# Grouped-query attention on one NeuronCore: the remainder tile of P transposed by DMA instead of TensorE in 101 of 128 steps

## The chip, the cores and the metric

The kernel runs on one core of a Trainium2 chip. The metric is device time in microseconds of one execution; for the kernel before, the median of three runs is given. A profile is one more execution with the hardware profiler on; its span runs from the first to the last instruction, and its own time is a little longer than the span. The engines are TensorE (PE in the profile, its weight loads PEld), VectorE (DVE), ScalarE (ACT), GpSimd (POOL) and SyncE (SP), which issues nearly all the DMA transfers. SPq is SyncE's sequencer.

## The reference

Two independent attention problems, A and B, have the same shapes; their outputs are joined along the last axis.

```python
B, Sq, D = 16, 80, 576
Hq, Hkv, Sk, Dh = 32, 16, 512, 128
...
q = (x @ wq).reshape(B, Sq, Hq, Dh).transpose(0, 2, 1, 3)
k = jnp.repeat(k_cache, 2, axis=1)
v = jnp.repeat(v_cache, 2, axis=1)
scores = jnp.einsum("bhqd,bhkd->bhqk", q, k) * (Dh ** -0.5)
p = softmax(scores, axis=-1)
o = jnp.einsum("bhqk,bhkd->bhqd", p, v)
return o.transpose(0, 2, 1, 3).reshape(B, Sq, Hq * Dh) @ wo
```

All tensors are bf16. Two query heads share one K/V head. Their 2 x 80 queries make 160 rows of scores by 512 keys for each of 16 batch entries, 16 K/V heads and 2 problems.

## The kernel before

**Units.** A unit U is one batch entry and four K/V heads of it; there are 64 units in each problem, 128 in all (`for U in range(NSU)`, line 573). A unit has four groups of 160 query rows. Since a tile has 128 partitions, each group gives one tile of its first 128 rows, and the last 32 rows of all four groups together make a fifth, the remainder tile. So a unit has five tiles k = 0 to 4: k = 0 is the remainder tile R, k = 1 to 4 are the A tiles. A step T = 5U + k is one tile.

**Loads.** SyncE loads K for a unit with a transposing DMA from HBM (`em_ldk`, line 582: 512 KB into one of NK buffers of `kT`) and V with a plain one (`em_ldv`, line 586: 512 KB into one of NV buffers of `v_sb`). It also loads pieces of wq (lines 487 and 490), wo (552) and x (422; 454 and 458 transposing, for problem B) and stores the output (775). SyncE's instructions run in order; each waits for the semaphores that it needs.

**A tile's way.** TensorE computes scores into PSUM (`em_qkr`, line 613, for the remainder tiles of a pair of units, four matmuls side by side; `em_qk`, line 627, for an A tile). VectorE takes the negated maximum (636), ScalarE the exponential with the row sum (640) into a slot of `p_sb`. When all five tiles of a unit have their sums, VectorE takes one reciprocal of the five columns (646; the groups are given by `RG`), and GpSimd scales each tile by it (649). TensorE transposes the tile with four matmuls against an identity (`em_tr`, 655), VectorE copies it from PSUM into `pT` (661 for the remainder tile, 663 for an A tile). Then TensorE multiplies with V (`em_pv`, 693: for each group four matmuls of 160 columns, 128 from its A tile and 32 from the remainder tile), and ScalarE copies the result to `oT` (708). Around this run the projection of Q (513, copied by 524 or 525) for the units to come, and the output projection (741, added up by 753, 764 or 769).

**Buffers.** `p_sb` has NPA = 9 slots for A tiles and NPR = 4 for remainder tiles, `pT` has NPT = 2 buffers of a unit each, `kT` NK = 6, `v_sb` NV = 4. PSUM has eight banks, given out by class (`BANKS`).

**Order.** The order of every engine's instructions is fixed when the program is built. Each operation has a due time (key) in steps, a duration, a list of what it reads and writes, and a stream; `_Sched.arrange` (line 115) is a list scheduler that walks through time, takes for each engine the ready operation with the lowest key among the heads of its streams, and gives out PSUM banks. For DMA it keeps one server, whose costs are constants (KC for a K load, VC for a V load, WQC for wq). `finalize` (229) turns the order into semaphore waits. LA is the number of steps by which the scores of a tile are due ahead of its transposition. Units are taken in pairs (GR = 2): the scores of both remainder tiles first, then the eight A tiles.

The layout of `pT` before is [128, buffer, group, j, 160], where j counts the four blocks of 128 keys:

```python
def em_ptev(e, k=k, gl=gl, vt=vt, pts=pts):
    if k == 0:
        return e.tensor_copy(pT[:, pts, :, :, 128:160],
                             psb[:, vt.phys, 0:512].rearrange("p (j g c) -> p g j c", j=4, g=4))
    return e.tensor_copy(pT[:, pts, gl, :, 0:128],
                         psb[:, vt.phys, 0:512].rearrange("p (j n) -> p j n", j=4))
```

Of the kernel before, what the change touches and what calls it, by code (L numbers as in the profile page):

```python
# [13 lines left out]
LA = 9  # L14
NK = 6
NV = 4
NPA = 9
NPR = 4
NPT = 2
# [3 lines left out]
KC = 3.1  # L23
# [5 lines left out]
VC = 1.75  # L29
# [11 lines left out]
RG = ((0, 1, 2, 3, 4),)  # L41
# [29 lines left out]
class _Op:  # L71
    __slots__ = ("engs", "eng", "key", "seq", "emit", "reads", "writes", "dsem", "stream", "dur", "lat", "cost",
                 "alloc", "pre", "start", "done", "mode",
# [3 lines left out]
class _Sched:  # L77
# [9 lines left out]
    def add(self, eng, key, emit, reads=(), writes=(), dsem=None, name="", stream=None, dur=0.1, lat=0.15,  # L87
            cost=0.0, alloc=(), mode=0):
        op = _Op()
        op.engs = (eng,) if isinstance(eng, str) else tuple(eng)  # L90
        op.eng = op.engs[0]
        op.key = float(key)
        op.seq = len(self.ops)
# [12 lines left out]
        op.pre = []  # L106
        op.start = op.done = None
        op.signals = False
        op.sidx = None
        op.waits = []  # L110
        op.clock = None
        self.ops.append(op)
        return op

    def arrange(self):
# [33 lines left out]
        mode = 0  # L149
# [5 lines left out]
        def ready(o):  # L155
            t = 0.0
            for d in o.pre:
                if d.done is None:
                    return None
                if not (d.eng == "pe" and o.engs[0] == "pe"):  # L160
                    t = max(t, d.done)
            if o.alloc:
                used = []
                for vb in o.alloc:
                    c = [(bank_free[b], n_, b) for n_, b in enumerate(BANKS[vb.cls])
                         if bank_free[b] is not None and b not in used]
                    if not c:
                        return None
                    b = min(c)
                    used.append(b[2])  # L170
                    t = max(t, b[0])
            return t

        while left:
            best = None
            for e in free:
                cand = []
                for n in by_eng[e]:
                    if at[n] < len(streams[n]):
                        o = streams[n][at[n]]  # L180
                        r = ready(o)
# [12 lines left out]
            dur = o.dur[e] if isinstance(o.dur, dict) else o.dur  # L194
            if e == "pe":
                if o.mode != mode:
                    st = max(st, now + 0.1)
                    mode = o.mode
            if o.alloc:
                used = []  # L200
                for vb in o.alloc:
                    b = min((bank_free[b], n_, b) for n_, b in enumerate(BANKS[vb.cls])
                            if bank_free[b] is not None and b not in used)[2]
                    used.append(b)
                    vb.phys = b
                for b in used:
# [91 lines left out]
def bass_concat_heads__gqa_block_cached__gqa_block_cached__near_ridge_kernel(  # L298
# [27 lines left out]
    with ExitStack() as es:  # L326
# [9 lines left out]
        pT = sb("pT", [128, NPT, 4, 4, 160], BF16)  # L336
# [14 lines left out]
                     + ["d_out%d" % i for i in range(NOSB)]  # L351
                     + ["d_k%d" % i for i in range(NK)] + ["d_v%d" % i for i in range(NV)])
# [115 lines left out]
        for goct in range(NG):  # L468
# [30 lines left out]
            for i in range(8):  # L499
                for c in range(2):  # L500
# [27 lines left out]
                    if prob:  # L528
# [3 lines left out]
                          writes=[R(vb, 0)], name="qp%d.%d.%d" % (goct, i, c), stream="Q",  # L532
# [40 lines left out]
        for U in range(NSU):  # L573
# [19 lines left out]
            vo = None  # L593
            for k in range(5):
# [47 lines left out]

                rg = [g_ for g_ in RG if k in g_][0]

# [28 lines left out]
                if k == rg[-1]:  # L673
                    S.add("dve", tg + 1.85, em_rcp, reads=[R(("rs", ss, k_), U) for k_ in rg],
                          writes=[R(("ri", ss, rg), U)], name="rcp%d" % T, stream="rcp", dur=0.10, lat=0.13)
# [3 lines left out]
                S.add("pe", t0, em_tr, reads=[R(("P", psl), ("n", T)), IDENT], writes=[R(vt, 0)],  # L679
                      name="tr%d" % T, stream="T", dur=_mm(4, 128), lat=0.2, alloc=[vt])  # L680
                S.add("dve", t0 + 0.44, em_ptev, reads=[R(vt, 0)], writes=pt_writes,
                      name="ptev%d" % T, stream="ptev", dur=0.33, lat=0.13)

                if k >= 1:
# [17 lines left out]
                    if gl % 2 == 1:  # L702
                        hb = 8 * (q % 2) + 4 * pr

                        def em_oev(e, vo=vo, hb=hb, row=half * NROW + bl * SQ):
# [6 lines left out]
                              stream="oev", dur=0.33)  # L712
# [4 lines left out]
        for prob in range(2):  # L717
            for hh in range(NPAIR):
                for half in range(NPP):
                    for n in range(NB_):  # L720
# [30 lines left out]
                        if hh == 0:  # L751
                            def em_ea(e, rb=rb, c3=c3, vb=vb):
# [5 lines left out]
                                  stream="oea", dur=0.30)  # L758
                        elif not last:
                            def em_em(e, rb=rb, c3=c3, vb=vb):  # L760
# [5 lines left out]
                                  stream="oeb", dur=0.38)  # L766
                        else:
# [4 lines left out]
                            def em_st(e, rb=rb, c3=c3, prob=prob, slot=slot):  # L772
# [6 lines left out]
                                  stream="oeb", dur=0.38)  # L779
# [75 lines left out]
```

## Time and profile before

| | |
|---|---|
| median of three runs | 790.78 us (790.53 to 791.19) |
| the profiled execution | 791.1 us |
| its span | 789.1 us, 21625 instructions |
| granted TensorE clock | 1.000 |
| share of the span on the chain that ended last | PE 87%; DVE 9% |
| line 655 in that chain | 16% |
| GpSimd scaling (649) | 640 of 692 ns |
| ScalarE exponentials (640) | 640 of 693 ns, 640 sum reads of 203 ns |
| VectorE maxima (636) | 640 of 677 ns |
| copies to pT (663 / 661) | 512 of 411 ns / 128 of 414 ns |
| reciprocals (646) | 128 of 179 ns |
| transposing matmuls (655), matmuls with V (693) | 2560, 2048 |
| K load, issue to landing | median 5.9 us (4.2 to 10.2) |
| V load, issue to landing | median 4.7 us (3.8 to 7.8) |
| DMA in all | 160.56 MB, mean 203 GB/s; q1 busy for 88.8% of 16 engines' span |

How to read it: a row of a group names the source line, engine, operation, output and inputs with shapes and count, then busy time and the mean length of one in ns, then the idle time of the engine before them and what ended it. Matmuls overlap, so the mean length of one is more than what it takes of the engine; the distance from one start to the next tells that. DMA shares are the time that packets took over 16 engines' time. A row of a timeline has the start, the length and the work, merged where the same work follows itself. For SyncE the length is that of issuing, with what holds it back.

### The profile page before, as it was taken

What the parts mean: (1) busy time and instruction counts of PE and PEld (TensorE: products, weight loads), DVE (VectorE), ACT (ScalarE), POOL (GpSimd) and SP (SyncE); (2) the same over time, 40 slices, a digit from 0 to 9 for tenths busy, and PEclk for the clock granted to TensorE, in tenths of its full rate; (3) what the DMA queues carried; (4) which work ended last, traced back from release to release, by engine and by line L of the source; (5) the groups of instructions that cost most, each with busy time, mean ns of one, the idle gap of its engine ahead of it and who ended that gap; (6) DMA issues with size and microseconds to landing.
All of it is one profiled execution on the core that took longest, in us unless ns stands there. A gap on an engine that the chain in (4) does not pass through costs nothing.

```text
span 789.1 us, 21625 instructions
## 1 busy us (share of the span) xinstructions
PE 782.3 (99%) x8258; PEld 577.7 (73%) x8258; DVE 687.8 (87%) x1553; ACT 613.9 (78%) x1741; POOL 432.1 (55%) x647
## 2 busy tenths in 40 slices
PE   9999999999999999999999999999999999999998
PEld 5677767777777777777777777777777777777776
DVE  4999999988888889889989999998888898989974
ACT  1779989888778889777787778888788877877852
POOL 1456666565564565565555555655555655654633
DMA  9999999999797899999988779998778876999620
GB/s 244 230 244 220 243 215 251 239 228 201 174 209 177 191 227 269 248 207 228 198 194 177 187 181 253 250 243 227 174 169 173 190 167 161 263 246 181 158 77 24
DMA packets 362085, 160.56 MB, mean 203 GB/s; under 512 B 276096, under 2 KB 358528, under 8 KB 361984
## 3 DMA queue, kind: packets, MB, share of 16 engines
q1 hardware_dynamic: 360768, 158.00, 88.8%
q8 instruction: 67, 1.10, 0.6%
q10 hardware_dynamic: 1216, 1.18, 0.4%
q14 instruction: 34, 0.28, 0.1%
HBM read 87.46 MB, written 2.95 MB: 115 GB/s over the span
## 4 chain that ended last, share of the span: by engine, by line
PE 87%; DVE 9%; SPq 1%; DMA 1%; ACT 1%; POOL 1%; issue 0%
PE ps L741 20%; PE ps L513 18%; PE ps L655 16%; PE ps L693 16%; PE ps L627 12%; DVE negmax L636 5%; PE ps L613 4%; DVE pT L663 2%; SPq L582 1%; DVE qT L525 1%; DMA wq_sb<-in_A_wq_dram 1%; POOL p_sb L649 1%; DVE pT L661 0%; ACT p_sb L640 0%; SPq L422 0%
## 5 line engine op out<-in xcount | busy, mean ns | idle before, releaser
L649 POOL TENSOR_SCALAR p_sb<-p_sb,rinv 128x512 bf16<-128x512 bf16 x640 | 429.7, 692 | 342.6 <-DVE rinv L646 342.3
L640 ACT ACTIVATE p_sb<-ps,negmax 128x512 bf16<-128x512 f32 x640 | 441.1, 693 | 84.0 <-DVE negmax L636 75.3
L636 DVE TENSOR_REDUCE negmax<-ps 128x1 f32<-128x512 f32 x640 | 428.4, 677 | 6.1 <-PE ps L627 2.0
L655 PE MATMUL ps<-ident,p_sb 128*128 128x128 bf16 x2560 | 240.7, 219 | 0.9 <-POOL p_sb L649 0.2
L663 DVE COPY pT<-ps 128x512 bf16<-128x512 bf16 x512 | 207.8, 411 | 19.9 <-PE ps L655 18.3
L693 PE MATMUL ps<-pT,v_sb 128*128 128x160 bf16 x2048 | 216.2, 233 | 0.5 <-ACT oT L708 0.3
L513 PE MATMUL ps<-xT,wq_sb 128*128 128x480 bf16 (+1 forms) x1280 | 211.7, 299 | 1.0 <-DVE xT L441 0.6
L655 PEld LDWEIGHTS ps<-ident,p_sb 128*128 128x128 bf16 x2560 | 177.2, 98 | 42.4 <-DVE pT L663 5.9
L693 PEld LDWEIGHTS ps<-pT,v_sb 128*128 128x128 bf16 x2048 | 158.5, 98 | 53.8 <-issue 11.9
L627 PE MATMUL ps<-kT,qT 128*128 128x512 bf16 x512 | 186.5, 379 | 0.0
L741 PE MATMUL ps<-wo_sb,oT 128*128 128x288 bf16 x1280 | 171.6, 286 | 0.5 <-ACT oT L708 0.5
L708 ACT CAST oT<-ps 128x320 bf16<-128x320 f32 x256 | 108.5, 425 | 55.0 <-PE ps L693 54.4
L513 PEld LDWEIGHTS ps<-xT,wq_sb 128*128 128x128 bf16 x1280 | 106.6, 98 | 59.2 <-issue 1.5
L741 PEld LDWEIGHTS ps<-wo_sb,oT 128*128 128x128 bf16 x1280 | 122.4, 98 | 35.0 <-ACT oT L708 1.4
L640 ACT ACTIVATION_READ_ACCUMULATOR p_sb<-ps,negmax 128x1 f32 x640 | 130.0, 203 | 0.0
L524 ACT ACTIVATE qT<-ps 128x160 bf16<-128x160 f32 (+1 forms) x164 | 65.9, 402 | 23.9 <-PE ps L513 23.1
L525 DVE TENSOR_SCALAR qT<-ps 128x480 bf16<-128x480 f32 (+1 forms) x92 | 51.7, 563 | 22.2 <-PE ps L513 21.3
L661 DVE COPY pT<-ps 128x512 bf16<-128x512 bf16 x128 | 53.0, 414 | 8.9 <-PE ps L655 7.4
L627 PEld LDWEIGHTS ps<-kT,qT 128*128 128x128 bf16 x512 | 48.6, 98 | 4.3 <-ACT p_sb L640 1.4
L769 DVE TENSOR_TENSOR osb<-ps,acc 128x288 bf16<-128x288 f32 x40 | 18.2, 456 | 25.4 <-PE ps L741 25.2
L613 PE MATMUL ps<-kT,qT 128*32 128x512 bf16 x512 | 39.6, 384 | 0.0
L646 DVE RECIPROCAL rinv<-rowsum 128x5 f32<-128x5 f32 x128 | 22.9, 179 | 9.9 <-ACT p_sb L640 9.8
(19 smaller groups left out, 48.2 us busy)
## 6 DMA issues: line engine op xcount, KB each, us to landing
v_sb<-in_A_v_cache_dram SPq DMA_DIRECT2D x64, 512.0 KB, 4.8
v_sb<-in_B_v_cache_dram SPq DMA_DIRECT2D x64, 512.0 KB, 4.7
wo_sb<-in_A_wo_dram SPq DMA_DIRECT2D x8, 576.0 KB, 6.7
wo_sb<-in_B_wo_dram SPq DMA_DIRECT2D x8, 576.0 KB, 7.1
wq_sb<-in_B_wq_dram SPq DMA_DIRECT2D x4, 1024.0 KB, 6.6
out_dram<-osb SPq DMA_DIRECT2D x40, 72.0 KB, 2.3
wq_sb<-in_A_wq_dram SPq DMA_DIRECT2D x2, 1024.0 KB, 6.3
wq_sb<-in_A_wq_dram ACTq DMA_DIRECT2D x2, 512.0 KB, 6.8
```

The lines of the kernel that those rows point to most:

```text
L513: last = e.matmul(ps[:, vb.phys, 0:n1 - n0], lhsT=wq_sb[:, wsl, ck, i * 128:(i + 1) * 128], rhs=xT[:, half, ck, n0:n1], start=(ck == 0), s ...
L524: return e.activation(dst, src, AF.Identity, scale=SCALE)
L613: last = e.matmul(ps[32 * g4:32 * g4 + 32, vb_.phys, :], lhsT=qT[:, qsl_, bl_, g4 * 160 + 128:g4 * 160 + 160], rhs=kT[:, ks_, :, g4 * 128: ...
L627: return e.matmul(ps[:, vb.phys, :], lhsT=qT[:, qsl, bl, gl * 160:gl * 160 + 128], rhs=kT[:, ks, :, gl * 128:(gl + 1) * 128], start=True, ...
L636: return e.tensor_reduce(negmax[:, si:si + 1], ps[:, vb.phys, :], axis=AX.X, op=AluOpType.max, negate=True)
L640: return e.activation(p_sb[:, psl, :], ps[:, vb.phys, :], AF.Exp, bias=negmax[:, si:si + 1], scale=1.0, accum_out=rowsum[:, ss, k:k + 1])
L649: return e.tensor_scalar(p_sb[:, psl, :], p_sb[:, psl, :], rinv[:, ss, k:k + 1], 1.0, op0=AluOpType.mult, op1=AluOpType.mult)
L655: last = e.transpose(psb[:, vt.phys, j * 128:(j + 1) * 128], p_sb[:, psl, j * 128:(j + 1) * 128], ident[:])
L663: return e.tensor_copy(pT[:, pts, gl, :, 0:128], psb[:, vt.phys, 0:512].rearrange("p (j n) -> p j n", j=4))
L693: last = e.matmul(ps[:, vo.phys, off:off + 160], lhsT=v_sb[:, vs, gl, j * 128:(j + 1) * 128], rhs=pT[:, pts, gl, j, :], start=(j == 0), st ...
L708: return e.copy(dst, src)
L741: last = e.matmul(ps[:, vb.phys, 0:DC], lhsT=oT[:, hi, rb * 128:(rb + 1) * 128], rhs=wo_sb[:, wi, c3 * DC:(c3 + 1) * DC], start=(hi == 0), ...
```

## The change

For units 24 to 124 (the condition takes U from 24 on and below 125, U % 2 being 0 or 1), the remainder tile is no longer transposed by TensorE and copied by VectorE. SyncE issues a transposing DMA from the tile's slot of `p_sb` in SBUF to its place in `pT`, also in SBUF. In these units the remainder tile has a reciprocal of its own, and the four A tiles share another. The layout of `pT` becomes [128, buffer, j, 5, 128]: for each block of keys four runs of 128 for the A tiles, cut as 32 rows of each of the four groups, and a fifth for the remainder tile. So a copy of an A tile writes runs of 32, and a matmul with V reads its 160 columns as five runs of 32. `pT` gets three buffers, K five instead of six, the A tiles of `p_sb` eight instead of nine, LA is 10 instead of 9, and two of the scheduler's DMA costs are lower.

The scheduler also changes how it gives out PSUM banks (the first bank of the class that is free at the time, tried for all banks that an operation needs, instead of the one that came free first), an operation may be put ahead of its key by `ahead` (used, with 6.0, for the new DMA alone: the others are 0.0), and the Q projection's matmuls also count as writers of `qT`.

```diff
-LA = 9
-NK = 6
+LA = 10
+NK = 5
 NV = 4
-NPA = 9
+NPA = 8
 NPR = 4
-NPT = 2
+NPT = 3
...
-KC = 3.1
+KC = 2.95
...
-VC = 1.75
+VC = 1.65
...
-RG = ((0, 1, 2, 3, 4),)
+RG = (((0, 1, 2, 3, 4),), ((0,), (1, 2, 3, 4)))
+RDMA = (24, 125)
+RPER = (0, 1)
+RSKIP = ()
+RDC = 0.75
+RDK = 3.0
+RDO = 6.0
+RDD = 0.8
...
+        def pick(vbs, now, used=()):
+            if not vbs:
+                return []
+            c = sorted((max(bank_free[b], now), n_, b) for n_, b in enumerate(BANKS[vbs[0].cls])
+                       if bank_free[b] is not None and b not in used)
+            for t, n_, b in c:
+                r = pick(vbs[1:], now, used + (b,))
+                if r is not None:
+                    return [(t, b)] + r
+            return None
...
-            k_, s_, r, o = min(((o.key, o.seq, r, o) for r, o in cand if r <= now + hold[e]), key=lambda x: x[:2])
+            k_, s_, r, o = min(((o.pri, o.seq, r, o) for r, o in cand if r <= now + hold[e]), key=lambda x: x[:2])
...
-        pT = sb("pT", [128, NPT, 4, 4, 160], BF16)
+        pT = sb("pT", [128, NPT, 4, 5, 128], BF16)
...
-                          writes=[R(vb, 0)], name="qp%d.%d.%d" % (goct, i, c), stream="Q",
+                          writes=[R(vb, 0)] + [R(("qT", qsl, bl, i), goct) for bl in range(b0, b0 + nb)],
+                          name="qp%d.%d.%d" % (goct, i, c), stream="Q",
...
+            rdma = RDMA[0] <= U < RDMA[1] and U % 2 in RPER and not any(a_ <= U < b_ for a_, b_ in RSKIP)
...
-                rg = [g_ for g_ in RG if k in g_][0]
+                rg = [g_ for g_ in RG[rdma] if k in g_][0]
...
                     if k == 0:
-                        return e.tensor_copy(pT[:, pts, :, :, 128:160],
-                                             psb[:, vt.phys, 0:512].rearrange("p (j g c) -> p g j c", j=4, g=4))
-                    return e.tensor_copy(pT[:, pts, gl, :, 0:128],
-                                         psb[:, vt.phys, 0:512].rearrange("p (j n) -> p j n", j=4))
+                        return e.tensor_copy(pT[:, pts, :, 4, :],
+                                             psb[:, vt.phys, 0:512].rearrange("p (j n) -> p j n", j=4))
+                    return e.tensor_copy(pT[:, pts, :, 0:4, gl * 32:gl * 32 + 32],
+                                         psb[:, vt.phys, 0:512].rearrange("p (j h c) -> p j h c", j=4, h=4))
+
+                def em_rtr(e, psl=psl, pts=pts):
+                    return e.dma_start_transpose(pT[:, pts, :, 4, :], p_sb[:, psl, :])
...
+                if k == 0 and rdma:
+                    S.add("sp", max(tg + RDK, 5.0 * (U - NPT) + 7.0), em_rtr, reads=[R(("P", psl), ("n", T))], writes=pt_writes, dsem="d_r%d" % pts,
+                          name="rtr%d" % T, stream="RT", dur=RDD, cost=RDC, ahead=RDO)
+                else:
+                    S.add("pe", t0, em_tr, reads=[R(("P", psl), ("n", T)), IDENT], writes=[R(vt, 0)],
+                          name="tr%d" % T, stream="T", dur=_mm(4, 128), lat=0.2, alloc=[vt])
+                    S.add("dve", t0 + 0.44, em_ptev, reads=[R(vt, 0)], writes=pt_writes,
+                          name="ptev%d" % T, stream="ptev", dur=0.33, lat=0.13, ahead=PTO)
...
                             lhsT=v_sb[:, vs, gl, j * 128:(j + 1) * 128],
-                                            rhs=pT[:, pts, gl, j, :], start=(j == 0), stop=(j == 3))
+                                            rhs=pT[:, pts, j, :, gl * 32:gl * 32 + 32], start=(j == 0), stop=(j == 3))
```

More of the change, by code (lines that the diff above doesn't have):

```diff
@@ L40 @@
 XDMA = True
-RG = ((0, 1, 2, 3, 4),)
+RG = (((0, 1, 2, 3, 4),), ((0,), (1, 2, 3, 4)))
[6 more added lines that the diff above has]
+RDD = 0.8
+PTO = 0.0
+OEO = 0.0
+OVO = 0.0
+QEO = 0.0
+RCO = 0.0
 NSS = 6
@@ L72 @@
     __slots__ = ("engs", "eng", "key", "seq", "emit", "reads", "writes", "dsem", "stream", "dur", "lat", "cost",
-                 "alloc", "pre", "start", "done", "mode",
+                 "alloc", "pri", "pre", "start", "done", "mode",
                  "deps", "signals", "sidx", "waits", "clock", "name")
@@ L87, in add @@
     def add(self, eng, key, emit, reads=(), writes=(), dsem=None, name="", stream=None, dur=0.1, lat=0.15,
-            cost=0.0, alloc=(), mode=0):
+            cost=0.0, alloc=(), mode=0, ahead=0.0):
         op = _Op()
@@ L92, in add @@
         op.key = float(key)
+        op.pri = op.key - ahead
         op.seq = len(self.ops)
@@ L153, in arrange, with ready @@
         hold = dict(pe=0.05, dve=0.02, act=0.02, pool=0.0, sp=0.0)
-        def ready(o):
+        def pick(vbs, now, used=()):
[8 more added lines that the diff above has]
+            return None
+        def ready(o, now):
             t = 0.0
@@ L162, in ready @@
             if o.alloc:
[L163 to L171, printed above, removed]
+                c = pick(o.alloc, max(t, now))
+                if c is None:
+                    return None
+                t = max([t] + [bank_free[b] for _, b in c])
             return t
@@ L180, in arrange @@
                         o = streams[n][at[n]]
-                        r = ready(o)
+                        r = ready(o, free[e])
                         if r is not None:
@@ L195, in arrange @@
             if e == "pe":
-                if o.mode != mode:
+                if o.mode and mode == 0 or o.mode != mode:
                     st = max(st, now + 0.1)
-                    mode = o.mode
+                mode = o.mode
             if o.alloc:
[L200 to L204, printed above, removed]
+                for vb, (_, b) in zip(o.alloc, pick(o.alloc, max(r, now))):
                     vb.phys = b
-                for b in used:
                     bank_free[b] = None
@@ L351, in bass_concat_heads__gqa_block_cached__gqa_block_cached__near_ridge_kernel @@
                      + ["d_out%d" % i for i in range(NOSB)]
+                     + ["d_r%d" % i for i in range(NPT)]
                      + ["d_k%d" % i for i in range(NK)] + ["d_v%d" % i for i in range(NV)])
@@ L674, in bass_concat_heads__gqa_block_cached__gqa_block_cached__near_ridge_kernel @@
                     S.add("dve", tg + 1.85, em_rcp, reads=[R(("rs", ss, k_), U) for k_ in rg],
-                          writes=[R(("ri", ss, rg), U)], name="rcp%d" % T, stream="rcp", dur=0.10, lat=0.13)
+                          writes=[R(("ri", ss, rg), U)], name="rcp%d" % T, stream="rcp", dur=0.10, lat=0.13, ahead=RCO)
                 S.add("pool", tg + 2.0 + 0.01 * k, em_nrm,
@@ L678, in bass_concat_heads__gqa_block_cached__gqa_block_cached__near_ridge_kernel @@
                       writes=[R(("P", psl), ("n", T))], name="nrm%d" % T, stream="pool", dur=0.674, lat=0.1)
[L679 to L682, printed above, removed]
+                if k == 0 and rdma:
[6 more added lines that the diff above has]
+                          name="ptev%d" % T, stream="ptev", dur=0.33, lat=0.13, ahead=PTO)
                 if k >= 1:
@@ L711, in bass_concat_heads__gqa_block_cached__gqa_block_cached__near_ridge_kernel @@
                               writes=[R(("oT", half, bl, q % 2, pr), (prob, q // 2))], name="oev%d.%d" % (U, pr),
-                              stream="oev", dur=0.33)
+                              stream="oev", dur=0.33, ahead=OEO)
         NB_ = NRT * NOC
@@ L757, in bass_concat_heads__gqa_block_cached__gqa_block_cached__near_ridge_kernel @@
                                   name="oea%d.%d.%d" % (prob, half, n),
-                                  stream="oea", dur=0.30)
+                                  stream="oea", dur=0.30, ahead=OVO)
                         elif not last:
@@ L765, in bass_concat_heads__gqa_block_cached__gqa_block_cached__near_ridge_kernel @@
                                   writes=[R(("acc", rb, c3), ver)], name="oem%d.%d.%d.%d" % (prob, hh, half, n),
-                                  stream="oeb", dur=0.38)
+                                  stream="oeb", dur=0.38, ahead=OVO)
                         else:
@@ L778, in bass_concat_heads__gqa_block_cached__gqa_block_cached__near_ridge_kernel @@
                                   writes=[R(("osb", slot), (prob, half, n))], name="oeb%d.%d.%d" % (prob, half, n),
-                                  stream="oeb", dur=0.38)
+                                  stream="oeb", dur=0.38, ahead=OVO)
                             S.add("sp", xe + 0.3, em_st, reads=[R(("osb", slot), (prob, half, n))],
```

## The prediction

> **What bounds the kernel now.** I read the page's busy times first, then its groups of instructions.
>
> ```profile
> PE 782.3 (99%) x8258; PEld 577.7 (73%) x8258; DVE 687.8 (87%) x1553; ACT 613.9 (78%) x1741; POOL 432.1 (55%) x647
> ...
> L655 PE MATMUL ps<-ident,p_sb 128*128 128x128 bf16 x2560 | 240.7, 219 | 0.9 <-POOL p_sb L649 0.2
> ```
>
> TensorE is busy 782.3 of 789.1 us; the next engine, VectorE, 687.8. A transposing matmul (L655) is given as 219 ns, but they overlap: 2,560 times 219 ns would be 561 us, and their busy time is 240.7. What one costs TensorE shows in TensorE's timeline (start, length, work):
>
> ```profile
> 307.41 0.39 PE L655 MATMUL ps<-ident,p_sb 128*128 128x128 bf16 x4
> 307.63 0.38 PE L627 MATMUL ps<-kT,qT 128*128 128x512 bf16 x1
> ```
>
> The four transposes of one tile start at 307.41, the next matmul at 307.63: one tile costs 0.22 us of TensorE. So TensorE's sequence of matmuls sets the end, and a tile taken from it is worth 0.22 us as long as nothing else makes TensorE wait.
>
> Next I asked how near the second resource is, the DMA engines that bring K and V. The view by stages gives for each stretch the busy times of the engines, then the granted clock, the DMA engines' share and GB/s:
>
> ```profile
> 40.00:183.00 143.00, 142.20 (x1538) 103.40 (x1531) 131.96 (x301) 125.63 (x361) 87.27 (x131) 1.00 1.08 233
> 183.00:736.00 553.00, 552.61 (x5904) 412.02 (x5902) 491.65 (x1108) 443.16 (x1261) 310.68 (x463) 1.00 0.91 206
> ```
>
> TensorE does not idle in the long stage (552.61 of 553), at clock 1.00 in both rows. The DMA engines stand at 1.08 in the early stage (packets overlap, so full load reads a little over 1) and at 0.91 in the later one. SyncE's own timeline says the same:
>
> ```profile
> 139.25 7.05 SPq L582 DMA_TRANSPOSE kT<-in_A_k_cache_dram  x2
> 146.35 0.59 SPq L586 DMA_DIRECT2D v_sb<-in_A_v_cache_dram  x1
> 146.98 4.09 SPq L582 DMA_TRANSPOSE kT<-in_A_k_cache_dram  x1
> 151.12 0.58 SPq L586 DMA_DIRECT2D v_sb<-in_A_v_cache_dram  x1
> 151.75 3.78 SPq L582 DMA_TRANSPOSE kT<-in_A_k_cache_dram  x1
> 155.57 1.13 SPq L586 DMA_DIRECT2D v_sb<-in_A_v_cache_dram  x2
> 156.76 8.21 SPq L582 DMA_TRANSPOSE kT<-in_A_k_cache_dram  x2
> 165.02 1.67 SPq L586 DMA_DIRECT2D v_sb<-in_A_v_cache_dram  x2
> 166.73 4.89 SPq L582 DMA_TRANSPOSE kT<-in_A_k_cache_dram  x1
> 172.04 0.37 SPq L586 DMA_DIRECT2D v_sb<-in_A_v_cache_dram  x1
> 172.47 4.26 SPq L582 DMA_TRANSPOSE kT<-in_A_k_cache_dram  x1
> 176.78 0.58 SPq L586 DMA_DIRECT2D v_sb<-in_A_v_cache_dram  x1
> 177.40 4.66 SPq L582 DMA_TRANSPOSE kT<-in_A_k_cache_dram  x1
> ...
> 202.47 2.32 SPq L582 DMA_TRANSPOSE kT<-in_A_k_cache_dram  x1
> 204.83 0.58 SPq L586 DMA_DIRECT2D v_sb<-in_A_v_cache_dram  x1
> 208.37 2.06 SPq L582 DMA_TRANSPOSE kT<-in_A_k_cache_dram  x1
> ```
>
> From 139.25 to 177.40 SyncE issues without a break and is held back: 8 K loads and 8 V loads in 38.15 us, 4.77 us a pair. That is what the DMA engines supply at full load. Later there are holes: after the V load of 204.83 the next K load starts at 208.37, because it waits for TensorE to free its K buffer. So from 183 us on the loads wait for TensorE. How far ahead they are, by the line of problem B's K loads in the view of line 582 (count, shortest, median and longest issue in ns, first and last start):
>
> ```profile
> L582 SPq DMA_TRANSPOSE kT<-in_B_k_cache_dram x64: 1310/2901/7492, 359.1 to 730.4; - x64
> ```
>
> The last K load starts at 730.4; the same view gives a median of 5.9 us from issue to landing, so it lands at 736.3; TensorE's timeline has its first reader (L613) at 756.50. It could come 20.2 us later for nothing.
>
> **The change, part by part.**
>
> *Removed.* The condition takes every unit from 24 to 124, even and odd: 101 remainder tiles. TensorE loses 101 x 0.22 = 22.2 us. VectorE loses 101 copies of 414 ns (row L661, like L663's 411), 41.8 us.
>
> *Added on VectorE.* 101 further reciprocals, 128x1 where the row L646 has 128x5 at 179 ns: at most 101 x 0.18 = 18 us, at least nothing. I take 18; VectorE ends at 688 - 42 + 18 = 664 us, well under TensorE. At the upper end nothing changes. ScalarE and GpSimd do the same 640 tiles as before; GpSimd's wait for the reciprocal (342 us in all) shows room there.
>
> *Same price, other place.* The pT layout changes: L663's copies now write runs of 32 elements and L693's matmuls read 160 columns in five such runs. For the copy the trace has both forms: runs of 32 in L661, 414 ns, against runs of 128 in L663, 411: nothing. For the matmul the nearest row is L627, whose 512 columns come in four runs of 128: started at 307.63, followed at 307.85, so 0.22 us for 512 columns, no visible loss. Bounds 0 and, at 4 ns for each of 2,048 matmuls, 8 us; I take 0.
>
> *LA 9 to 10, NK 6 to 5, NPA 9 to 8, the bank picker.* These move the order, not the amount of work. The scores run one tile earlier, a K buffer is released about a unit (6 us) later relative to its load. K loads were up to some 25 us early in the quiet stage, so I take 0; it costs up to 6 us where they are late already. Below nothing: the few TensorE gaps left before the last stage could close, at most 782.3 against 789.1 us, of which most is the start; 2 us.
>
> *Added on SyncE and the DMA engines.* 101 transposes of 128 KB each, a quarter of a K load. No row shows a transfer from SBUF to SBUF. Nearest row: K loads issued back to back while held back, 7.05 us for two at 139.25, so about 3.4 us each. Bounds: a quarter of the shortest K issue (1.31 us), 0.33 us, and a whole one, 1.31 us, if most of it does not shrink with the size. I take a little under the quarter of 3.4 us, since the pair of 139.25 queued behind V loads too: 0.78 us, 79 us in all.
>
> One rule speaks against this step. The Trainium skill, "VectorE: DVE Perf Modes", section "The three transpose paths", lists 1309 ns for a 128x128 transpose by DMA and 390 ns on TensorE. This trace differs for both: 0.055 us a block at TensorE's pace (0.22 over four), and 0.21 us a block for a K load (3.4 us over its 16 blocks). By the page's figure a remainder tile would take an estimated 5.2 us of DMA, 529 us in all, and the kernel would run hundreds of us longer. I go by the rows.
>
> *What hides the 79 us.* Only the spare time of the DMA engines from 183 to 736 us. Two readings. By SyncE: 93 K loads follow from 183.41 on, 93 x 4.77 = 444 us; the other transfers, at K's 3.4 or V's 4.77 - 3.4 = 1.4 us per 512 KB, are 12 wo pieces 19, four wq loads 13, two x transposes 11, some 20 stores 4, together 47; 444 + 47 = 491 of 547 us, 56 spare. By the stages: (1 - 0.91/1.08) x 553 = 87 us. The middle is 71.
>
> *Sum.* The last K load lands at 736.3 + 79 - 71 = 744. TensorE wants it at 756.5 - 22.2 = 734. So TensorE waits about 10 us somewhere before, and this wait is the new price. The profiled execution took 791.1 us around its span of 789.1: 791.1 - 22.2 + 10 = 778.9. The median of the runs, 790.78, lies 0.3 lower, so **779 us**.
>
> *The new wait.* On SyncE a transpose waits for GpSimd's normalization, and nearly each also for the PV matmuls (L693) of three units before, which free its pT buffer. In the changed order two units read V, R, K, R, V, K: a K and a V load stand behind each R. Their readers have the leads above as cover. PV itself now waits for the landing. In TensorE's timeline of before, PV of unit 71 ended at 447.50 and PV of unit 74 began at 462.07, 14.6 us later; the transpose needs its place behind one K issue (2 to 5 us) and about 5.9 us to land, 11 at most. When K issues take 7 us, as at some places, little is left.
>
> **The rivals.**
>
> *Hidden entirely.* If an R costs 0.6 us, its share by bytes of a pair (128 KB of 1 MB, 4.77/8), 61 us fit into 71 spare and no wait appears: 791 - 22 = 769; with closed gaps 767. For it: SyncE stood idle in many holes after 183 us. Against it: holes are wanted evenly, and the stages with wo, wq and x loads have none.
>
> *The DMA engines become the bound (slower).* Place: the K loads of the crowded stages, from about unit 50 on. Price: at 0.88 us an R (a quarter of 3.5) and 56 us spare the last K load lands at 736.3 + 89 - 56 = 769, 35 us after it is wanted: 791 - 22 + 35 = 804. It turns slower once transposes minus spare pass 20 us, so at 0.90 us an R with the middle spare, or 0.75 with the lower one. For it: the SyncE reading of 4.77 us a pair, and one buffer of K less. Against it: the stages' reading.
>
> *It does not do what it says.* If the matmuls read runs of 32 more slowly, say 7 ns on each of 2,048, PV takes 14 us back and with the wait of the forecast nothing is left: 779 + 14 = 793. Row L627 speaks against it.
>
> **How the numbers follow.** Forecast, part of the gain given back to DMA waits: 0.46 (its own range 771 to 788). Hidden: 0.25. DMA the bound: 0.23, of which 0.02 ends beside the old time. Reads slower: 0.06. The range runs from 766, just under the hidden case, to 801, inside the slower one, leaving out about 0.05 above and little below; the far ends of an R's price, 0.33 us (33 us in all: hidden) and 1.31 us (132 us: a wait of 63 and 832 us), lie in it and above it. A difference under 0.2% (1.6 us) could not be told from none. Faster: 0.46 + 0.25 with a small loss to "same", 0.70; same 0.04; slower 0.26.
>
> **What would show it.** TensorE's transposes 404 fewer and 22 us less of them on the chain; 101 more issues on SyncE, 128 KB each; DMA share in the long stage near 1.05; the holes on SyncE gone; new waits of L613 or L627 for kT, or of L693 for pT, some 10 us in all. No such waits: the hidden case. Waits above 20 us, named kT: the bound has moved. Waits on pT: the landing is late, which I count small. Wrong altogether if PV's pace leaves 0.28 us a group (307.13 to 307.41), or if VectorE becomes the longest.

## The result, and the profile after

The changed kernel takes 812.41 us (median of four runs, 811.29 to 817.73) against 790.65 for the kernel before beside it (790.42 to 791.19): a ratio of 1.0287, 95% interval 1.0242 to 1.0333. It is slower by 21.8 us where 779 was forecast. The profiled execution took 812.9 us, with a span of 811.2.

The page of the kernel after, its busy times, queue q1, the engines' shares of the chain that ended last, and some groups (busy, mean ns of one, then idle time before them and what ended it):

```profile
PE 775.9 (96%) x7854; PEld 554.5 (68%) x7854; DVE 665.0 (82%) x1554; ACT 613.1 (76%) x1740; POOL 432.8 (53%) x647
...
q1 hardware_dynamic: 415712, 171.26, 97.4%
...
PE 67%; DVE 17%; ACT 7%; DMA 7%; issue 1%; POOL 1%; SPq 1%; ACTq 0%
...
L680 DVE COPY pT<-ps 128x512 bf16<-128x512 bf16 x512 | 207.7, 412 | 36.2 <-PE ps L672 34.1
L717 PE MATMUL ps<-pT,v_sb 128*128 128x160 bf16 x2048 | 202.5, 234 | 16.6 <-DMA pT<-p_sb 4.1
...
L672 PE MATMUL ps<-ident,p_sb 128*128 128x128 bf16 x2156 | 204.2, 220 | 4.8 <-POOL p_sb L666 2.8
...
L663 DVE RECIPROCAL rinv<-rowsum 128x1 f32<-128x1 f32 (+1 forms) x229 | 37.3, 164 | 17.3 <-ACT p_sb L657 17.0
```

TensorE lost its 404 transposing matmuls (2560 to 2156) and is busy 6 us less, but in a longer span: 96% where it was 99%. The matmuls with V (L717, before L693) had 0.5 us of idle time before them and now have 16.6; what ended the largest single part of it, 4.1 us, was the new transfer. The part of TensorE in the chain fell from 87% to 67%.

The view by stages of the kernel after (PE, PEld, DVE, ACT, POOL busy; then granted clock, DMA share, GB/s):

```profile
40.00:183.00 143.00, 141.23 (x1503) 101.69 (x1501) 130.96 (x304) 122.87 (x352) 87.95 (x131) 1.00 1.06 234
183.00:736.00 553.00, 529.03 (x5356) 379.24 (x5355) 455.35 (x1074) 430.68 (x1226) 302.52 (x450) 0.99 1.01 217
```

The early stage is nearly as before: TensorE idles 1.8 us in it where it idled 0.8, and experiment 1 below, without the transfers, has 1.7. In the long one TensorE now idles 24 us where it idled 0.4, and the DMA share went from 0.91 to 1.01.

SyncE's timeline of the kernel after, in a stretch without other transfers:

```profile
542.70 3.25 SPq L598 DMA_TRANSPOSE kT<-in_B_k_cache_dram  x1
545.99 1.27 SPq L684 DMA_TRANSPOSE pT<-p_sb  x1
547.31 0.57 SPq L602 DMA_DIRECT2D v_sb<-in_B_v_cache_dram  x1
547.92 3.45 SPq L598 DMA_TRANSPOSE kT<-in_B_k_cache_dram  x1
551.48 1.21 SPq L684 DMA_TRANSPOSE pT<-p_sb  x1
552.73 1.50 SPq L602 DMA_DIRECT2D v_sb<-in_B_v_cache_dram  x1
554.60 3.49 SPq L598 DMA_TRANSPOSE kT<-in_B_k_cache_dram  x1
```

Two units, K, R and V each, take from 542.70 to 554.60, 5.95 us a unit; ten units from 542.70 (the tenth next K load starts at 600.64) make 5.79. A pair of K and V alone took 4.77 at full load, so an R (the new transfer) costs 1.0 to 1.2 us of the supply. The K load behind an R is still held 3.25 to 3.5 us. From 183 to 736 us SyncE's holes of more than 0.2 us add up to 158 us in the kernel before and to 5 in this one. Its last K load and its R lines, from the views of their source lines (shortest, median, longest issue in ns; first and last start), with who waited for an R (us, times) and the time from issue to landing, read:

```profile
L598 SPq DMA_TRANSPOSE kT<-in_B_k_cache_dram x64: 1387/3410/5917, 374.9 to 763.5; - x64
```

```profile
L684 SPq DMA_TRANSPOSE pT<-p_sb x101: 1189/1212/3190, 154.4 to 772.9; - x101
...
who waited for it (us, times):
  ACT p_sb L657: 9.1, 9
  PE ps L717: 4.1, 4
  PEld ps L717: 3.8, 3
...
DMA to landing us min/median/max: 2.4/3.8/8.9
```

The last K load starts at 763.5 where it was 730.4, 33.1 us later, and lands 0.31 us ahead of its reader where there were 20. An R never takes SyncE less than 1.19 us. Not only the matmuls with V wait for it. An R also reads its tile's slot in `p_sb`, one of four, and the exponential (L657) of the remainder tile four units later may not write there before; ScalarE waited 9.1 us for that, in 9 places.

How this reaches TensorE, at one place. First SyncE, then TensorE (the bracket is idle time and what ended it), both of the kernel after:

```profile
404.58 3.11 SPq L598 DMA_TRANSPOSE kT<-in_B_k_cache_dram  x1
407.79 1.21 SPq L684 DMA_TRANSPOSE pT<-p_sb  x1
```

```profile
410.41 0.38 PE L644 MATMUL ps<-kT,qT 128*128 128x512 bf16 x1
412.52 1.21 PE L717 MATMUL ps<-pT,v_sb 128*128 128x160 bf16 x15 [1.72 <-DMA pT<-p_sb]
```

This R's tile had been scaled by 392.89, and its place in pT was free at 395.61. Behind other loads it was issued at 407.79 only, 12.2 us later, landed at 412.47, and TensorE's next matmul waited 1.72 us for it. Matched to its tile by the program's order, each of the 101 R gives such a time from ready to issued: the median is 9.7 us, the longest 20.2.

**An account of TensorE's time.** For every matmul I took the time from its start to the next start, less the pace of its form (0.22 us for 512 columns); what is left is a stall. Before: 15.4 us in all, 1.3 of it ahead of L693. After: 59.0, of which 23.0 ahead of L717, 9.1 ahead of L672, 14.2 ahead of the scores L630 and L644 (6.2 before), 5.9 ahead of L765. So 791.1 (the profiled execution of before) - 22.2 saved + 43.6 more stalls = 812.5, where 812.9 was measured. The sum has to close nearly by itself, since the time from the first matmul to the last is made of paces and stalls; that it does shows that the matmuls kept their paces. So the saving is there, and the added stalls are twice as large. By the program's order some 16 of the 23.0 us ahead of L717 end with the landing of an R; all the waits that end with the landing of a K load come to some 3 us. About 3.4 us of the stalls come from two stretches at half the granted clock (last section); they aren't the cause, for the run of 811.29 us had a granted clock of 1.000.

### The profile page after: what moved, and what is told of

Read it like the earlier page. It is cut to its first block, busy times and chain, and to the rows that moved or that the text cites. A ratio compares the mean times of both kernels' runs of the same rounds, so it can differ in the third digit from the quotient of the medians.

```text
span 811.2 us, 20842 instructions
## 1 busy us (share of the span) xinstructions
PE 775.9 (96%) x7854; PEld 554.5 (68%) x7854; DVE 665.0 (82%) x1554; ACT 613.1 (76%) x1740; POOL 432.8 (53%) x647
## 3 DMA queue, kind: packets, MB, share of 16 engines
q8 instruction: 64, 1.05, 0.5%
## 4 chain that ended last, share of the span: by engine, by line
PE 67%; DVE 17%; ACT 7%; DMA 7%; issue 1%; POOL 1%; SPq 1%; ACTq 0%
PE ps L765 16%; PE ps L528 14%; PE ps L717 13%; DVE negmax L653 10%; PE ps L672 10%; PE ps L644 8%; ACT p_sb L657 5%; DMA pT<-p_sb 5%; DVE pT L680 4%; PE ps L630 3%; DVE qT L540 1%; DMA wo_sb<-in_B_wo_dram 1%; ACT oT L732 1%; DMA out_dram<-osb 1%; ACT qT L539 1%
## 5 line engine op out<-in xcount | busy, mean ns | idle before, releaser
L657 ACT ACTIVATE p_sb<-ps,negmax 128x512 bf16<-128x512 f32 x640 | 439.8, 696 | 76.2 <-DVE negmax L653 59.8
L653 DVE TENSOR_REDUCE negmax<-ps 128x1 f32<-128x512 f32 x640 | 425.6, 678 | 34.9 <-PE ps L630 18.3
L680 DVE COPY pT<-ps 128x512 bf16<-128x512 bf16 x512 | 207.7, 412 | 36.2 <-PE ps L672 34.1
L717 PE MATMUL ps<-pT,v_sb 128*128 128x160 bf16 x2048 | 202.5, 234 | 16.6 <-DMA pT<-p_sb 4.1
L672 PE MATMUL ps<-ident,p_sb 128*128 128x128 bf16 x2156 | 204.2, 220 | 4.8 <-POOL p_sb L666 2.8
L717 PEld LDWEIGHTS ps<-pT,v_sb 128*128 128x128 bf16 x2048 | 152.3, 98 | 61.4 <-ACT p_sb L657 8.5
L644 PE MATMUL ps<-kT,qT 128*128 128x512 bf16 x512 | 185.2, 380 | 2.1 <-ACT p_sb L657 1.9
L672 PEld LDWEIGHTS ps<-ident,p_sb 128*128 128x128 bf16 x2156 | 151.8, 98 | 51.7 <-DVE pT L680 10.4
L765 PE MATMUL ps<-wo_sb,oT 128*128 128x288 bf16 x1280 | 175.6, 288 | 3.6 <-ACT p_sb L657 2.0
L765 PEld LDWEIGHTS ps<-wo_sb,oT 128*128 128x128 bf16 x1280 | 122.4, 98 | 40.0 <-ACT oT L732 2.2
L657 ACT ACTIVATION_READ_ACCUMULATOR p_sb<-ps,negmax 128x1 f32 x640 | 133.7, 209 | 0.0
L644 PEld LDWEIGHTS ps<-kT,qT 128*128 128x128 bf16 x512 | 48.6, 98 | 15.4 <-ACT p_sb L657 9.1
L663 DVE RECIPROCAL rinv<-rowsum 128x1 f32<-128x1 f32 (+1 forms) x229 | 37.3, 164 | 17.3 <-ACT p_sb L657 17.0
L630 PE MATMUL ps<-kT,qT 128*32 128x512 bf16 x512 | 40.0, 388 | 2.2 <-ACT qT L539 0.8
L777 ACT COPY acc<-ps 128x288 f32<-128x288 f32 x40 | 16.1, 408 | 7.3 <-PE ps L765 7.0
```

The source lines that it names most:

```text
L630: last = e.matmul(ps[32 * g4:32 * g4 + 32, vb_.phys, :], lhsT=qT[:, qsl_, bl_, g4 * 160 + 128:g4 * 160 + 160], rhs=kT[:, ks_, :, g4 * 128: ...
L644: return e.matmul(ps[:, vb.phys, :], lhsT=qT[:, qsl, bl, gl * 160:gl * 160 + 128], rhs=kT[:, ks, :, gl * 128:(gl + 1) * 128], start=True, ...
L653: return e.tensor_reduce(negmax[:, si:si + 1], ps[:, vb.phys, :], axis=AX.X, op=AluOpType.max, negate=True)
L657: return e.activation(p_sb[:, psl, :], ps[:, vb.phys, :], AF.Exp, bias=negmax[:, si:si + 1], scale=1.0, accum_out=rowsum[:, ss, k:k + 1])
L672: last = e.transpose(psb[:, vt.phys, j * 128:(j + 1) * 128], p_sb[:, psl, j * 128:(j + 1) * 128], ident[:])
L680: return e.tensor_copy(pT[:, pts, :, 0:4, gl * 32:gl * 32 + 32], psb[:, vt.phys, 0:512].rearrange("p (j h c) -> p j h c", j=4, h=4))
```

## The experiments

In each expectation the forecast's mechanism and its rivals are named as they stood then. In the diffs the line before is that of the changed kernel.

**1. The change without its transfers.** All other edits stay; every remainder tile goes through TensorE.

```diff
-RDMA = (24, 125)
+RDMA = (0, 0)
```

> The changed kernel with the new transfer switched off for all units; new pT layout, LA, NK, NPA, NPT and the scheduler's edits stay. Theory A (each remainder transfer takes a fixed 1.16 us of the K and V loads' supply), theory S (the DMA engines run empty for some 1.5 us whenever a plain load follows a transposing one) and theory L (the transfers land late in their queue, supply is enough) all say: as before, 787 to 793 us. Theory O (the other edits cost the time): 805 us or more.

Measured: 791.07 us (790.44 to 791.79), ratio 0.9999 (0.9989 to 1.0008). The view by stages of this run:

```profile
183.00:736.00 553.00, 552.21 (x5907) 413.20 (x5905) 488.47 (x1100) 448.69 (x1270) 313.44 (x466) 1.00 0.92 205
```

TensorE is busy 552.21 of 553 us at the old DMA share. The layout of pT with its runs of 32, the buffers, LA and the bank picker cost and bring nothing together; the transfers alone make the difference. What this run leaves is also the yardstick for SyncE: 444.4 us of issuing K, 71.3 of V, and 150 us of holes from 183 to 736.

**2. Half of the transfers** (even units, 51).

```diff
-RPER = (0, 1)
+RPER = (0,)
```

> Remainder transfer in even units only, 51 instead of 101. Theory A: 51 x 1.16 = 59 us, less than the 71 us spare before, so no wait: 791 - 11 = 780 us (777 to 784). Theory S: about the same, as no change of kind is added. Theory L: half the loss stays, 791 - 11 + 22 = 802 us. Theory O: above 800 us.

Measured: 787.07 us (785.31 to 788.31), ratio 0.9946 (0.9927 to 0.9964), faster than before. TensorE's stalls are 23.7 us, 7.1 of them ahead of L717. The result lies between the free case (777 to 784) and the late one (802), nearer to the free one: what is too much at 101 mostly fits at 51, even spread over all stages. The pT waits left are in the stages with wo, wq, x and output transfers, where one R landed 9.4 us after its issue.

**3. The same bytes as a plain copy.** The data in that part of pT is then not transposed.

```diff
-                    return e.dma_start_transpose(pT[:, pts, :, 4, :], p_sb[:, psl, :])
+                    return e.dma_start(pT[:, pts, :, 4, :], p_sb[:, psl, :].rearrange("p (j n) -> p j n", j=4))
```

> The 101 transfers move the same bytes to the same place as plain copies, not transposed (so the output is not the attention's). Theory A, if the price is that of a transposing instruction: SyncE's issue falls from 1.2 to about 0.5 us, time near 770 us. Theory S: a plain copy among the K loads adds one change of kind per unit, so 101 x 1.5 us more of empty DMA engines on top: 830 us or more. If the price is that of the bytes: as changed, 812 us.

Measured: 780.79 us, one run. The new transfer's line, and the long stage, of this run:

```profile
L684 SPq DMA_DIRECT2D pT<-p_sb x101: 593/620/1876, 154.5 to 737.2; - x101
...
DMA to landing us min/median/max: 2.3/3.4/9.6
```

```profile
183.00:736.00 553.00, 547.67 (x5645) 397.76 (x5643) 479.53 (x1136) 450.17 (x1285) 320.62 (x475) 1.00 1.05 229
```

A plain transfer occupies SyncE for 0.62 us, half of a transposing one, lands about as late, and 101 of them leave 27.6 us of stalls: 31.6 us faster than the changed kernel, though the DMA engines' share is higher (1.05 against 1.01). So neither the bytes nor the latency nor the packets' time make the change slow; that the transfer transposes does. The time is 11 us above the 770 of the expectation. A plain transfer is still issued some 5 us (median) after it could be, but no matmul with V waits for one.

**4. V loads in pairs.** To see if it is the switching from a transposing to a plain transfer that costs, the V loads of two units are issued together (K R K R V V).

```diff
-            S.add("sp", 5.0 * U - VK, em_ldv, writes=[R(("V", vs), U)],
-                  dsem="d_v%d" % vs, name="ldv%d" % U, stream="V", dur=0.45, cost=VC)
+            if U % 2 == 0:
...
+                S.add("sp", 5.0 * U - VK, em_ldv2, writes=[R(("V", vs), U), R(("V", vs + 1), U + 1)],
+                      dsem="d_v%d" % vs, name="ldv%d" % U, stream="V", dur=0.9, cost=2 * VC, nd=2)
```

> As changed, but the V loads of two units are issued one right after the other, so that the queue reads R K R K V V instead of R K R V K V; same loads, same bytes, half the changes from transposing to plain. Theory S: 64 changes fewer, 64 x 1.5 = 96 us of DMA time back, more than the 48 us of lateness: 768 to 776 us. Theory A: the number of transfers is the same, so 807 to 817 us. Theory L: 807 us or more, since a remainder transfer now waits behind two K or V loads.

Measured: 810.42 us (807.65 to 813.0), ratio 1.0243 (1.0214 to 1.0272). Counted over all of SyncE's transfers, there are 174 changes between the two kinds instead of 256, and the time is the same within its spread. The kernel before has 244 and experiment 1 has 252, so the change hardly adds any. The switch isn't the price; between the other two theories, which both allowed 807 us and more, this run doesn't decide.

**5. V loads from another engine**, ScalarE and, in a second kernel, GpSimd.

```diff
-            S.add("sp", 5.0 * U - VK, em_ldv, writes=[R(("V", vs), U)],
+            S.add("act", 5.0 * U - VK, em_ldv, writes=[R(("V", vs), U)],
```

> As changed, with the V loads issued from ScalarE's queue instead of SyncE's; same transfers and bytes, all transposing ones still on SyncE. Theory Q (what runs out is SyncE's one queue: each transfer starts there only after the one before has been issued, at 1.2 us for a remainder transfer and some 3.4 us for a K load that is held back): SyncE is relieved of 88 us of V issues and two streams fill each other's gaps, 766 to 782 us, less what ScalarE loses by 128 issues of 0.6 us. Theory D (the DMA engines themselves are full): 807 to 817 us.

> The same with the V loads on GpSimd's queue, which stands idle 45 % of the time. Theory Q: 766 to 785 us. Theory D: 807 to 817 us.

Measured: ScalarE 805.45 us (801.01 to 811.92), ratio 1.0182 (1.0126 to 1.0239); GpSimd 839.18, one run, at a granted clock of 0.981. Both lie outside what either theory gave. SyncE's timeline of the ScalarE variant in a crowded stage:

```profile
433.62 1.21 SPq L684 DMA_TRANSPOSE pT<-p_sb  x1
434.88 9.49 SPq L598 DMA_TRANSPOSE kT<-in_B_k_cache_dram  x1
444.47 1.51 SPq L684 DMA_TRANSPOSE pT<-p_sb  x1
446.02 5.75 SPq L598 DMA_TRANSPOSE kT<-in_B_k_cache_dram  x1
```

SyncE is freed of 88 us of V issues and has 53 us of holes again, and an R is issued 2.7 us (median) after it could be, where it was 9.7. But single K loads are held up to 9.49 us, and what is issued lands later: an R after 5.1 us (median), where it was 3.8, a K load after 7.0, where it was 6.1. Stalls are 53.3 us. The Trainium skill, "DMA: Bandwidth & Descriptors", section "Issuing engines are not separate DMA queues", says that a second issuing engine saves only its sequencer's time, since all of them share the same DMA engines. These 7 us for 88 us of issues moved agree. So SyncE's queue is not the only limit: close behind it are the transfers themselves, whoever issues them.

**6. Half of the bytes.** Each R brings two of the four blocks of keys, 64 KB; the other two of the remainder tile in pT are stale.

```diff
-                    return e.dma_start_transpose(pT[:, pts, :, 4, :], p_sb[:, psl, :])
+                    return e.dma_start_transpose(pT[:, pts, 0:2, 4, :], p_sb[:, psl, 0:256])
```

> As changed, but each of the 101 transfers brings only two of the tile's four 128x128 blocks, 64 KB (the other half of the remainder tile in pT is left as it was, so the output is not the attention's). Price per transfer, not per byte: issue stays 1.2 us, time 805 to 815 us. Price per byte: issue 0.6 us, half of 117 us is less than the spare time, 769 to 785 us.

Measured: 809.76 us (808.94 to 810.58), ratio 1.023 (1.021 to 1.0251). The R line of this run, and its long stage:

```profile
L684 SPq DMA_TRANSPOSE pT<-p_sb x101: 1170/1192/2523, 154.5 to 769.9; - x101
```

```profile
183.00:736.00 553.00, 528.12 (x5382) 378.39 (x5380) 457.27 (x1077) 431.71 (x1230) 304.34 (x451) 1.00 0.93 207
```

Half the bytes bring 2.6 us. An R still takes SyncE 1.19 us, while the DMA share is down to 0.93, nearly that of before (0.91): the kernel is nearly as slow with DMA engines that are not full. The price hangs on the number of transposing transfers, hardly on their size.

**7. Transfers only where there is room.** 48 of them, none in the stages with wo, wq, x and most output transfers.

```diff
-RSKIP = ()
+RSKIP = ((46, 66), (78, 96), (110, 125))
```

> As changed, but without the transfer in units 46 to 65, 78 to 95 and 110 to 124, where wo, wq, x and the stores share the queue: 48 transfers remain, all in quiet stretches. If the loss is the crowded stages (lateness behind other transfers): TensorE saves 48 x 0.22 = 10.6 us and nothing is given back, 780 us (778 to 784). If the loss is spread evenly over all transfers (48 of 101): 791 - 10.6 + 0.48 x 44 = 801 us.

Measured: 784.2 us (780.53 to 787.43), ratio 0.9895 (0.9853 to 0.9937): the lowest median of the kernels that leave nothing out. The two runs at a granted clock of 1.000 took 780.53 and 781.77, those at 0.996 took 786.64 and 787.43. The profiled one is that of 786.64: at one place TensorE waited 3.10 us for a K load (of unit 57, which has no R) and then ran 6.8 us at half clock, 6.5 us lost together. Less that place, this run comes to the 780 of the expectation; the other three were not profiled. Only 1.0 us of stalls is ahead of L717, though an R takes longer to land than in the changed kernel:

```profile
L684 SPq DMA_TRANSPOSE pT<-p_sb x48: 1194/1212/2110, 154.5 to 656.7; - x48
...
DMA to landing us min/median/max: 2.4/4.2/6.9
```

From ready to issued an R takes 1.8 us here in the median, 5.3 at most, against 9.7 and 20.2. So it is not the landing itself (4.2 us here, 3.8 there) that makes the matmuls with V wait, but how long the R stands in SyncE's queue. This run has fewer transfers as well as other places; experiment 2, with about as many over all stages, tells the two apart: 787.07 us, with 7.1 us of stalls ahead of L717. By the medians the place is worth some 3 us, and going from 51 to 101 transfers 25.

**8. Fewer still**: 28, the even units of the quiet stretches; and **9.**, the 101 and the 48 transfers with the planner's constants for an R at its measured price.

```diff
-RPER = (0, 1)
-RSKIP = ()
+RPER = (0,)
+RSKIP = ((46, 64), (79, 93), (111, 125))
```

```diff
-RDC = 0.75
+RDC = 1.2
...
-RDD = 0.8
+RDD = 1.2
```

> 28 transfers: the even units, and only in the quiet stretches (units 24 to 44, 64 to 78, 94 to 110). Supply theory (each transfer costs a fixed 1.2 us of the loads, and hurts only where the spare is used up): all 28 find room, no wait for pT beyond 1 us, and the time is that of before minus 28 x 0.22 = 6.2 us: 784.5, no better than the 48 transfers of the quiet stretches (784.2), since these pay 10.6 us of which some 4 were given back. Rival (any mixed order of R, K and V costs something of its own, whatever the spare): 787 or more.

> All 101 transfers as in the changed kernel, but the order is planned with 1.2 us for a transfer instead of 0.75 (its duration too, 1.2 instead of 0.8). Theory of the order (the planner priced a transfer too low, so it put readers too early and loads too late; an order made for the true price would do): 790 or less. Supply theory (101 x 1.16 us do not fit into 71 us of spare, in whatever order): 803 to 815, since the same transfers must be brought in; a better order can only take away the waits for pT that come from a transfer standing behind a load, a few us.

> The 48 transfers of the quiet stretches with the order planned for 1.2 us a transfer. Supply theory: the transfers have room there, so 782 to 785, at best before minus 48 x 0.22 = 10.6, 780. Theory of the order: the 4 us that were given back at 48 transfers come from the plan, so 780 or a little less.

Measured: 28 transfers 785.34 us (785.16 to 786.03), ratio 0.9932 (0.9917 to 0.9947), stalls 17.1 us. 101 transfers planned at 1.2 us: 823.96 (822.0 to 828.54), ratio 1.0406 (1.0389 to 1.0423), worse than the change and 9 us above its expectation. 48 planned at 1.2 us: 785.44 (785.02 to 786.39), ratio 0.9933 (0.9918 to 0.9948), no better than experiment 7, and above the 782 to 785 that was expected. The groups of the 101 planned at 1.2 us, and what waited for an R in that run:

```profile
L717 PE MATMUL ps<-pT,v_sb 128*128 128x160 bf16 x2048 | 197.3, 234 | 7.5 <-DVE osb L793 3.2 <-ACT p_sb L657 1.0 <-DVE qT L540 1.0
L672 PE MATMUL ps<-ident,p_sb 128*128 128x128 bf16 x2156 | 202.2, 220 | 15.4 <-POOL p_sb L666 11.8 <-DVE pT L680 3.4
```

```profile
who waited for it (us, times):
  ACT p_sb L657: 14.7, 10
```

A plan with the true price no longer puts the R matmuls too early (stalls ahead of L717 fall from 23.0 to 13.8 us), but the stall comes back ahead of other lines (L672: 9.1 to 23.9), 73.4 us in all, and the last K load is 15 us later still. Neither order brings in what the supply lacks. Part of why this one is worse is in the last fence: the exponentials wait 14.7 us for an R to leave its slot in `p_sb`, where it was 9.1, and the tiles behind them are late. The longest of these waits, 4.99 us, ends at 337.44; TensorE stood still for 3.19 us beside it and ran the 10.2 us from 339.3 on at half clock. In experiments 3 and 7 no exponential waits for an R. The rest was not followed.

**Two accounts over the runs.** Saved is 0.22 us for each R; the sum is 791.1 - saved + (stalls - 15.4), beside the profiled execution's own time. The next columns are SyncE's issuing over the whole run: of the R, and what K and V took more than in experiment 1, which has 150 us of holes from 183 to 736.

| kernel | R | saved | stalls | sum | profiled | R issue | K, V more | together |
|---|---|---|---|---|---|---|---|---|
| changed | 101 | 22.2 | 59.0 | 812.5 | 812.9 | 132.6 | 28.3, 16.6 | 178 |
| half the bytes | 101 | 22.2 | 57.1 | 810.6 | 810.6 | 134.3 | 34.9, 7.8 | 177 |
| plain copy | 101 | 22.2 | 27.6 | 781.1 | 780.8 | 67.1 | 56.3, 6.0 | 129 |
| even units | 51 | 11.2 | 23.7 | 788.2 | 787.2 | 74.2 | 26.4, 5.2 | 106 |
| quiet stretches | 48 | 10.6 | 21.6 | 786.7 | 786.6 | 62.2 | 40.9, 8.4 | 112 |
| quiet, even | 28 | 6.2 | 17.1 | 786.6 | 786.0 | 34.3 | 21.8, 4.1 | 60 |

The sums meet the measured times to 1 us in every row (in the others to 1.6: V in pairs 808.1 and 807.7, V from ScalarE 806.7 and 807.7, planned at 1.2 us 826.9 and 828.5). The new issuing stays under the 150 us of holes in the four kernels that beat the one before, and goes over them by about 28 us in the other two. Their last K load was issued 27 and 24 us later than in experiment 1. Of the kernels outside the table, the sum is 97 us for the 48 planned at 1.2 us (785.44), 158 for V in pairs (810.42, last K load 24 us later) and 195 for the 101 planned at 1.2 us (823.96, 42 later). So this sum tells faster from slower in all of them, but not by how much: V in pairs goes over by 8 us only.

## Why the prediction was wrong

**The step that failed is the price of an R**, "I take a little under the quarter of 3.4 us ...: 0.78 us, 79 us in all". It scaled a K load by its bytes. An R has a quarter of a K load's bytes, but takes 1.19 us of SyncE at least, with half of the bytes too (experiment 6), and 1.0 to 1.2 us of the supply's pace, 101 to 121 us in all. The upper bound, a whole shortest K issue of 1.31 us, "if most of it does not shrink with the size", was the near one: that row already showed a transposing transfer's issue, and the scaling threw it away. In the prediction's own sum, with all else as it stood, 1.0 to 1.2 us an R gives 801 to 821 us, with the measured 812 in the middle.

**The spare time was about right.** By the pace above, with 33 us of lateness and 101 to 121 us of transfers, it comes to 68 to 88 us; 56 to 87 was said and 71 taken. "The last K load lands at ... 744" became 770.5.

**The slower rival came true.** "DMA engines become the bound" had the last K load land at 769 (770.5 measured) and 804 us. Its price of 0.88 us was low and its spare of 56 us too; that the two cancelled is luck. Its name is only half right: by experiments 3 and 6 the DMA engines' share does not decide (1.05 at 781 us, 0.93 at 810), the number of transposing transfers does. Its place, from about unit 50 on in the crowded stages, is borne out only in part: in experiment 2 the waits for pT lie there, but the step from 51 to 101 transfers costs far more than the place (25 against 3 us). It fell 8 us short; the waits for pT, which it did not price, are the next item.

**The new wait was counted small and is over a third of the loss.** "11 at most of 14.6" added one K issue to the landing. Both were right alone (landing median 3.8 us, 8.9 at most), but an R stands in a queue that is never empty, and is issued 9.7 us in the median after it could have been, where one K issue of 2 to 5 us was allowed for. Ahead of L717 the stalls went from 1.3 to 23.0 us, half of the 43.6 added, and some 16 us of them end with the landing of an R. A second wait isn't in the prediction at all: that of the exponentials for the slot in `p_sb` that an R still reads, 9.1 us of ScalarE's time here and 14.7 in experiment 9. Experiment 7 shows the same transfer without either wait where the queue has holes. The sign to look for had been given, waits above 20 us, but for kT; they are mostly for pT (some 16 us, against 3 for kT).

**What held.** TensorE's 0.22 us a tile (the matmuls kept their paces in every row), VectorE's end (664 said, 665.0 measured; the reciprocals at 164 ns, all forms), the copies in runs of 32 (412 ns), reads in runs of 32 at no cost and the other edits at nothing (experiment 1 for all of them together).

**Left open.** Whether the 1.2 us of a transposing transfer is spent in SyncE's issuing alone or also in the path of the transfers behind it: with V moved away, SyncE had holes and the R left its queue sooner, but K loads were held longer and all landed later instead (experiment 5). Issuing the R from another engine, which might tell, was not tried.

## What to carry to other kernels

Price a small transfer by the shortest issue of its kind in the trace, not by its share of a big one's bytes; for 101 R that is 1.19 against 0.78 us, and a forecast gain of 12 us came out as a loss of 22. A resource with spare time on average has room for only so much of a new load: 51 transfers over all stages brought 0.5%, 101 cost 3%. The stages where its queue has holes are the better place: 48 transfers put there brought 1%. When an engine's wait is moved onto a queue that never runs empty, count the time from when the transfer could go to when it is issued, not only its flight, and list all that waits for it: those who need its result, and those who need the place it reads from.

## What the runs showed of the hardware that was not expected

A transposing transfer from SBUF to SBUF takes the issuing engine 1.19 us (median) with 64 KB and 1.21 with 128 KB, and a plain one of 128 KB 0.62.

The granted TensorE clock halved after short stalls. The kernel after, around such a place (same columns as before):

```profile
300.00:309.50 9.50, 7.51 (x76) 5.37 (x75) 9.18 (x23) 9.07 (x27) 6.93 (x11) 1.00 1.20 313
309.80:313.20 3.40, 3.40 (x20) 2.43 (x18) 0.56 (x2) 0.19 (x2) 0.00 (x0) 0.50 0.74 158
313.50:320.00 6.50, 6.50 (x74) 4.60 (x72) 5.41 (x14) 4.83 (x14) 4.08 (x6) 1.00 1.08 255
```

In the first stretch TensorE idles 2 us, 1.99 of it in one piece; for the 3.4 us from 309.80 on the clock is 0.50, and 20 matmuls run in them, against 74 in the 6.5 us of the third row. It happened twice in this kernel (again for 3.4 us from 579.4 on, after TensorE had idled 0.49 and 1.52 us), and for 6.8 us beside 3.10 us of idling in experiment 7. So a wait of 2 us cost about 3.7. An idle time of 1.72 us, at 412.52, wasn't followed by it. The Trainium skill, "TensorE: Matmul & The Clock Gate", section "HAM oscillation — how this bites in real kernels", warns of idle gaps above some 3.4 us; here idle times of 1.52 and 1.99 us were followed by the half clock, so the measurement sets a lower mark. Without a run that stalls TensorE on purpose it stays a sequence seen in the traces, not a shown cause.

V loads issued by GpSimd gave 839.18 us (one run), 34 more than the same loads issued by ScalarE; why was not followed.
